# A fused sigmoid attention and token MLP on one core: a new order of steps, loads, casts and copies, seven casts on VectorE, one quadrant group fewer

## The chip, the cores and the metric

One core of a Trainium2 chip. The metric is the device time of one launch in microseconds (us): the median of several runs. Beside it stands the profile of one execution, whose span runs from the first to the last instruction.

## What is computed

Inputs are q, k, v of 8 batches, 12 heads, 448 tokens, head dimension 64 (fp32), and three weights. First comes attention with a sigmoid in place of the softmax, then a token-mixing MLP whose mixing weights are made from the attention's output:

```
attn  = sigmoid(q @ k.T / 8 - log(448))            # per batch and head
x     = (attn @ v) as [8, 448, 768]
wq, wk = x @ w_q, x @ w_k                          # hidden size 64
mixed = (wq @ wk.T / 8) @ x                        # per batch
out   = relu(mixed) @ w_out
```

The kernel computes in bf16 with fp32 sums and orders the MLP's products as wq @ (wk.T @ x), so that no 448 x 448 matrix is made there.

## The kernel before

**Units.** Four heads of one batch make a quad; there are 24 quads, three to a batch. A quad has 7 score steps, 168 in all. A score step is four 64x64-tiled matmuls of 448 columns on TensorE (line 121 records every matmul, line 124 every transpose), which fill one pair of PSUM banks, and one sigmoid of 128x896 on ScalarE (L331), which frees the pair and writes one of 16 slots of `at`. A value step multiplies one slot with `v` and sums into another pair; the seventh value step of a quad ends with a copy to `xt` (L355).

**From load to score.** SyncE issues the loads of q, k, v (448 KB each) and of w_out into a ring of six buffers `ld0` to `ld5`; a load goes out when the buffer's former content has been cast. Casts to bf16 run on GpSimd (L211 for q and k, L221 for v and the first q and k), a few on VectorE. Then q and k are transposed in one of three ways: on TensorE with a copy back by VectorE (L292, L300), or on VectorE alone. Of the latter, the plan letters `c` and `d` take one 128x448 STREAM_TRANSPOSE each for q and k (L271), after GpSimd has rearranged the cast tile with five copies (L167, L170, L173). The letters `r`, `s`, `z` do without the rearrangement: two 128x448 transposes (L264) and a quadrant group of four 32x448 ones (L251).

**MLP.** For each batch `xt` is transposed to `xn` (plan letters x, X, y, Y; X and Y as 7 whole 128x128 transposes, x and y as 28 of 64x64; y and Y with the copy by ScalarE, L384 or, in the tail, halves at L382); w and W multiply with w_q and w_k (the cast weights are `wqk`, four 64x384 casts, L754); N transposes the result to `wkn` (L449); U makes `tmp` (L462), M the mixed and rectified `mx` (L467, L469), O the output (copies at L601 and L646, the last at L599 and L555 in the function `middle`). w, X and part of O use all 128x128 cells, the rest 64x64 tiles.

**What sets the order.** All is written out by hand: `PLAN` is one letter per step (S score, P or p value step, the letters above, D one store of an output tile, C a copy of w_out to the other half, 1 the next cast that `ORDER` marks with a dot, on VectorE), `BANKS` gives the PSUM pair (0 to 3) or single bank (a to h) of each step that takes one, `ORDER` the order of the loads (q1 is quad 1's q; w0 are w_q and w_k, w1 to w6 are w_out). Each engine runs its instructions strictly in the order in which the plan issues them; a cast without a dot goes to GpSimd as soon as its buffers are planned free.

```
        if t in "12":
            cast_one("vs"[int(t) - 1])
            continue
```

Of the kernel before, what the change touches and what calls it, by code (L numbers as in the profile page):

```python
# [17 lines left out]
def kernel(  # L18
# [22 lines left out]
    NB = D // 2  # L41
# [6 lines left out]
    def pool(name, bufs, **kw):  # L48
# [15 lines left out]
    pairs = [banks[:, 2 * n : 2 * n + 2] for n in range(4)]  # L64
    pairs16 = [banks16[:, 2 * n : 2 * n + 2] for n in range(4)]
    BANKS = (
        "abcd0123200233111020302312031203101031021g2012020120h1g21320"
        "132123103103213012302g01h20h1g2031a32102312g12h1201321gh0210"
        "12h01210321g201321g2h01gh201g20132cd302c302302131e301230ef31"
        "0ef3102102c302d320d320123cd20gh120g102310g102hg102312gh10210"  # L70
        "ef130210ef1302120120320312321031021021321a310320321320120123"
        "020210320120c3210210312"
    )
    given = list("".join(BANKS))
    held = set()
# [1 line left out]
    def bank2():  # L77
        n = int(given.pop(0))
        assert not held & {2 * n, 2 * n + 1}
        held.update({2 * n, 2 * n + 1})  # L80
        return n, pairs[n], pairs16[n]
# [7 lines left out]
    def release(fb):  # L89
        gone = {2 * fb, 2 * fb + 1} if isinstance(fb, int) else {"abcdefgh".index(fb)}  # L90
        assert gone <= held
        held.difference_update(gone)
# [16 lines left out]
    def ld_next():  # L109
        nld[0] += 1  # L110
        return lds[(nld[0] - 1) % 6]
# [8 lines left out]
    def mm(*args, **kw):  # L120
        products.append(nc.tensor.matmul(*args, **kw))  # L121
# [6 lines left out]
    COPY = dict(v=nc.vector.tensor_copy, s=nc.scalar.copy, g=nc.gpsimd.tensor_copy)  # L128

    def xt(u, j):  # L130
# [5 lines left out]


    PLAN = (
        "SSFKESSES1EEqESDD1DESjPPppSpDpPDSSSqS1kSpPPSqSpSkSDPPSPSxSxr"
        "sSWwDDDDSSwzDPpSPppSpPSrSwSwWsSPpXSPNpSpPPSUSqSzMSSkpSpPpSMS"  # L140
        "ppPSSxSxMScPpSdPSpppSSPwWwrWSSXWDWSSosOSNPpPSpppzPSSOOSxSrPP"
        "ppSUSsppzPSoSOSoSoSppMpSPPPPSSWOWWWScSdxWODSMDWSOSxCOSMppScP"
        "DppSPPDSodDoSpxPDPDSCPrPSpDSPOOSNSsSOoDzOOSUSXcSPdpPSSpPPSPo"
        "OWSMSwowWMSSOwWCScpppSxpdpSpPSOoMSPPcDSPPpSpSPOoNSSSdDOoDOOp"
        "xDSPpPxSPpPDSuwcWwdSSMWOoSMSDwwOOSDxpPSPrPSmPpPDooNDSDSosoOz"
        "oSDDSxOOSUDpSDPPPDSPpcDSPoDODSSSodOoOSPMpSPPPSPPSwWwoScMSdOw"
        "wSSWOONSPMPcpSPPPPSSOodXSOSxoSoxSOppSpcUPSPpPSoOSdSxOOSPPPmp"
        "pPSPoSoMmOSOLScllLSLLSDodODSONxOPSpcpdpDPSPSPoOSoSOSOoSUSoSO"
        "SpPPpp1SoSOpSPOSOyppPMpPpplMlmlxlLlxOoONooUoOMmooOmooOoOOOOO"
        "oOOOOooOo"  # L150
    )
    PLAN = "".join(PLAN)
    KIND = ["a"] + [t for t in PLAN if t in "qacr"]
# [384 lines left out]
    def middle(w, us, k, part, fb, ps):  # L538

        x = part // 2  # L540
        for c in range(part % 2 * NC // 2, (part % 2 + 1) * NC // 2):
            for u in us:
                st = mxs[w].rearrange("p (c u s) -> p c u s", u=2, s=S)[:, c, u, 3 * NP : 4 * NP]
                mm(
                    ps[HALF[u], x, 0:NB], st, wout16[:, c, x * NB : (x + 1) * NB],
                    start=(c == 0), stop=(c == NC - 1),
                )
        if part % 2:
            if not x:
                ot[0] = ld_next()[:, 0:D]  # L550
            o = ot[0][:, x * NB : (x + 1) * NB]
            half = NB // 2
            for y in range(2):
                cols = slice(y * half, (y + 1) * half)
                COPY["vs"[y]](out=o[:, cols], in_=ps[:, x, cols])  # L555
            rows = out[2 * w : 2 * w + 2].rearrange("u (p i) d -> (u p) i d", i=NI)[:, NI // 2, x * NB : (x + 1) * NB]
            if x:
                for y in range(2):
                    (nc.sync, nc.scalar)[y].dma_start(out=rows[HALF[y]], in_=o[HALF[y]])
            else:  # L560
                nc.sync.dma_start(out=rows, in_=o)
        if part < 3:
            opened.append((w, us, k, part + 1, fb, ps))
        else:
            release(fb)

    def out_pair(act, tail):
# [7 lines left out]
        if len(us) == 2 and w == MIXED:  # L575
            middle(w, us, k, part, fb, ps)
            return
# [101 lines left out]
    def cols(r):  # L679
        return slice(r.start * HD, r.stop * HD)  # L680
# [8 lines left out]
        out=ident, in_=ident, compare_op=ALU.not_equal, fill=1.0, base=0,  # L689
# [4 lines left out]
    for _ in range(31):  # L694
# [1 line left out]


    ORDER = (
# [5 lines left out]
    )  # L704
    BEHIND = {}
    BY = {"s": [], "v": []}
# [76 lines left out]
    for t16, t32, r, e in (  # L783
# [3 lines left out]
            out=t16[:, r].rearrange("p i b d -> p b i d"),  # L787
            in_=t32[:, :, cols(r)].rearrange("p b (i d) -> p b i d", d=HD),
# [3 lines left out]
    def tr_part(nm, t16, r, e, tiled=False):  # L792
# [19 lines left out]
        out=k016[:, K3].rearrange("p i b d -> p b i d"), in_=k0[:, :, cols(K3)].rearrange("p b (i d) -> p b i d", d=HD),  # L812
# [10 lines left out]
    for t in PLAN:  # L823
        pump_loads()
        pump()
        if t in "EF":
            fb, ps, _ = bank2()
# [49 lines left out]
        elif kind == "C":  # L877
            for y in range(2):
                nc.sync.dma_start(
                    out=wout16[HALF[y], NC + 2 * c : NC + 2 * c + 2, :], in_=wout16[HALF[1 - y], 2 * c : 2 * c + 2, :],  # L880
# [5 lines left out]
        elif kind == "M":  # L886
            u, x = divmod(c, NC // 2)
# [42 lines left out]
```

## Time and profile before

| | |
|---|---|
| time, median of 3 runs | 186.0 us (185.35 to 186.64) |
| span of the profiled execution | 183.1 us |
| between that span and the median | 2.9 us |
| TensorE, matmuls | 170.9 us busy, 93% |
| ScalarE | 159.4 us, 87% |
| VectorE | 134.4 us, 73% |
| GpSimd | 117.1 us, 64% |
| granted TensorE clock | 1.00 |

The profiled execution has no timed run of its own; its span lies 2.9 us under the median. Busy shares are averages over stages with different limits. The rows of the profile name line, engine, operation, tile written and tiles read, then the count, the busy time and the mean of one; PE is TensorE's matmuls, PEld its weight loads, DVE VectorE, ACT ScalarE, POOL GpSimd, SP SyncE. The end of a matmul is modelled and matmuls overlap, so a PE row that shows no gap may still hide waits of a tenth or two of a microsecond; the starts of rows are measured.

### The profile page before, as it was taken

Reading aid. Unit: us, or ns where it says so; the run is one execution under the profiler, and the core shown is the slowest. Engines: PE = TensorE matmul, PEld = TensorE weight load, DVE = VectorE, ACT = ScalarE, POOL = GpSimd, SP = SyncE. Lnnn points to the kernel's source line nnn. Section 1 sums busy time; section 2 is a strip of 40 time slices with the busy share of each in tenths; the row PEclk is TensorE's granted clock in tenths of the full one; section 3 lists DMA queues with packets and bytes.
Section 4 is the critical chain, followed back from the end, with each engine's and each line's share of the span. In section 5 each row is a group of like instructions: output and inputs, shape, how many; then the busy total and the mean of one; then the engine's idle time right before and its main releaser. Section 6 shows DMA issues by size and latency. Waiting matters only on the chain.

```text
span 183.1 us, 8403 instructions
## 1 busy us (share of the span) xinstructions
PE 170.9 (93%) x3617; PEld 113.1 (62%) x3618; DVE 134.4 (73%) x205; ACT 159.4 (87%) x207; POOL 117.1 (64%) x156
## 2 busy tenths in 40 slices
PE   7887789899999999999999999999999999999990
PEld 7544435544564565555556546556788898888970
DVE  2545699988998898988758876789786885693310
ACT  4699999999999999999999999899989979964330
POOL 1228988998799996699999928999999400000000
PEclk9999999999999999999999999999999999999999
DMA  5999999969998769899889998997983333333686
GB/s 175 349 383 286 332 381 397 392 234 310 372 401 330 258 209 312 297 280 366 311 236 300 350 324 278 355 361 261 292 304 94 87 98 95 90 90 81 139 219 173
DMA packets 24261, 48.51 MB, mean 265 GB/s; under 512 B 3872, under 2 KB 16416, under 8 KB 24224
## 3 DMA queue, kind: packets, MB, share of 16 engines
q1 hardware_dynamic: 24000, 47.69, 78.4%
q8 instruction: 28, 0.46, 1.0%
q10 hardware_dynamic: 224, 0.30, 0.5%
q14 instruction: 9, 0.07, 0.1%
HBM read 35.78 MB, written 11.01 MB: 256 GB/s over the span
## 4 chain that ended last, share of the span: by engine, by line
PE 75%; ACT 13%; DMA 4%; issue 2%; DVE 2%; SPq 1%; ACTq 0%
PE banks L121 72%; ACT at L331 13%; DMA ld<-in_v_dram 4%; PE banks L124 4%; DVE xt L355 1%; DVE mx L469 1%; SPq L197 1%; DVE v L221 0%; DVE xn L384 0%; SPq L684 0%; SPq L682 0%; SPq L683 0%; DVE ld L555 0%; ACT ld L555 0%; ACTq L331 0%
## 5 line engine op out<-in xcount | busy, mean ns | idle before, releaser
L331 ACT ACTIVATE at<-banks 128x896 bf16<-128x896 f32 x168 | 141.1, 946 | 5.7 <-PE banks L121 5.2
L121 PE MATMUL banks<-wout,mx 64*64 64x384 bf16 (+2 forms) x816 | 66.2, 324 | 0.7 <-issue 0.6
L121 PE MATMUL banks<-qk 64*64 64x448 bf16 x672 | 61.5, 358 | 3.6 <-ACT at L331 2.8
L211 POOL CAST qk<-ld 128x896 bf16<-128x896 f32 x38 | 44.6, 1191 | 9.7 <-issue 7.3
L121 PEld LDWEIGHTS <-mx 64*64 64x64 bf16 (+2 forms) x816 | 39.6, 105 | 17.4 <-issue 6.9
L121 PE MATMUL banks<-at,v 64*64 64x448 bf16 x672 | 47.2, 351 | 0.9 <-ACT at L331 0.4
L121 PEld LDWEIGHTS <-qk 64*64 64x64 bf16 x672 | 27.1, 105 | 24.4 <-issue 18.0
L355 DVE CAST xt<-banks 128x896 bf16<-128x896 f32 x23 | 25.0, 1086 | 7.9 <-PE banks L121 6.0
L121 PEld LDWEIGHTS <-v 64*64 64x64 bf16 x672 | 23.7, 106 | 7.0 <-issue 1.4
L469 DVE TENSOR_SCALAR mx<-banks 128x896 bf16<-128x896 f32 (+1 forms) x21 | 19.9, 956 | 5.0 <-PE banks L121 4.2
L221 POOL CAST v<-ld 128x896 bf16<-128x896 f32 x22 | 20.7, 948 | 1.5 <-DMA ld<-in_v_dram 1.1
L271 DVE STREAM_TRANSPOSE qk<-qk 128x448 f32<-128x448 f32 x26 | 16.0, 630 | 0.1
L384 DVE COPY xn<-banks 128x896 bf16<-128x896 bf16 x21 | 13.1, 624 | 3.5 <-PE banks L124 2.6
L251 DVE STREAM_TRANSPOSE qk<-qk 32x448 f32<-32x448 f32 x24 | 15.3, 636 | 0.6
L170 POOL COPY qk<-qk 32x448 uint32<-32x448 uint32 x26 | 14.4, 554 | 1.6
L173 POOL COPY qk<-swap 32x448 uint32<-32x448 uint32 x26 | 14.4, 554 | 1.5
L121 PE MATMUL banks<-xt,wqk 64*64 64x448 bf16 (+1 forms) x84 | 13.8, 353 | 0.2 <-ACT at L331 0.2
L646 DVE COPY o<-banks 128x384 f32<-128x384 f32 x17 | 9.4, 553 | 3.4 <-PE banks L121 2.6
L124 PEld LDWEIGHTS <-xt 64*64 64x64 bf16 (+1 forms) x588 | 9.8, 108 | 3.1 <-issue 1.5
L124 PE MATMUL banks<-ident,xt 64*64 64x64 bf16 (+1 forms) x588 | 10.4, 194 | 0.2
L121 PE MATMUL banks<-wqk,tmp 64*64 64x448 bf16 (+3 forms) x72 | 8.7, 291 | 0.0
L121 PE MATMUL banks<-wq,tmp 64*64 64x448 bf16 (+2 forms) x72 | 8.4, 292 | 0.0
(67 smaller groups left out, 136.0 us busy)
## 6 DMA issues: line engine op xcount, KB each, us to landing
ld<-in_q_dram SPq DMA_DIRECT2D x24, 448.0 KB, 6.1
ld<-in_v_dram SPq DMA_DIRECT2D x24, 448.0 KB, 5.6
ld<-in_k_dram SPq DMA_DIRECT2D x23, 448.0 KB, 6.1
out_dram<-o SPq DMA_DIRECT2D x38, 192.0 KB, 4.9
out_dram<-ld SPq DMA_DIRECT2D x14, 192.0 KB, 2.8
ld<-in_moe_w_out_dram SPq DMA_DIRECT2D x6, 384.0 KB, 5.1
wout<-wout SPq DMA_DIRECT2D x6, 192.0 KB, 4.9
out_dram<-o SPq DMA_DIRECT2D x4, 96.0 KB, 1.9
```

The source lines that it names most:

```text
L121: products.append(nc.tensor.matmul(*args, **kw))
L124: products.append(nc.tensor.transpose(*args, **kw))
L170: eng.tensor_copy(out=w[lo, 1], in_=w[hi, 0])
L173: eng.tensor_copy(out=w[hi, 0], in_=z[lo])
L211: COPY[e](out=f[:, :, "qk".index(nm)].rearrange("p e i d y -> p e y i d"), in_=ld.pop((nm, n)).rearrange("p (y i e d) -> p e y i d", y=2, ...
L221: COPY[e](out=t16.rearrange("p i b d -> p b i d"), in_=ld.pop((nm, n)).rearrange("p b (i d) -> p b i d", i=NI),)
L251: nc.vector.transpose(out=qk[n][other : other + 32, h].rearrange("p t i n -> p (t i n)").bitcast(F32), in_=w[own : own + 32, 1 - h],)
L271: nc.vector.transpose(out=qk[n][:, t].rearrange("p t i n -> p (t i n)").bitcast(F32), in_=w)
L331: nc.scalar.activation(dst, src, ACTF.Sigmoid, bias=attn_bias, scale=attn_scale)
L355: COPY[eng](out=xt(u, j), in_=ps)
L384: COPY[eng](out=xn, in_=ps)
L469: nc.vector.tensor_scalar(dst, ps, moe_scale, 0.0, ALU.mult, ALU.max)
```

## The change

`PLAN`, `BANKS` and `ORDER` are written anew. Counted by letter: casts marked for VectorE go from four (q1, v0, k2, v23) to seven (q2, q3, w0, k19, v17, v18, v21); the quads with a quadrant group go from six to five (quad 17 is now of the kind c, d); three `xn` copies of the body (of batches 0, 5 and 6) go from VectorE to ScalarE (in the tail, behind the last score, each copy is split between the two whatever its letter); whole transposes (X, Y) from four to five, and 64x64 ones from 20 to 19; w and W are dealt anew, so that one pair of copies of `wq` leaves ScalarE for GpSimd. The letters S, P, D, M, N, U, C and the output steps stay the same in number. In the function `middle` the last two column halves of the output are no longer copied in two pieces each, one by VectorE and one by ScalarE; the first half is copied whole by VectorE, the second whole by ScalarE. Lines behind that place move up by three, so that L754 becomes L751, L601 L598, L646 L643.

```
-        "abcd0123200233111020302312031203101031021g2012020120h1g21320"
+        "abcd23001220113323310203120302301303c0312102g102012h0g123120"
...
-        "SSFKESSES1EEqESDD1DESjPPppSpDpPDSSSqS1kSpPPSqSpSkSDPPSPSxSxr"
-        "sSWwDDDDSSwzDPpSPppSpPSrSwSwWsSPpXSPNpSpPPSUSqSzMSSkpSpPpSMS"
...
+        "SSFKESSESEEqDESjSDSSS1SPqppPSPkPSPSPS1SppqSDkpPSpPSXSryESS1S"
+        "SswzDWppPpSpPPSwDDWSDSSwrWXpNSDPspDDpSPPPSUzSSSMSqkSpPSPDPMS"
...
-            half = NB // 2
-            for y in range(2):
-                cols = slice(y * half, (y + 1) * half)
-                COPY["vs"[y]](out=o[:, cols], in_=ps[:, x, cols])
+            COPY["vs"[x]](out=o, in_=ps[:, x, 0:NB])
...
-        ".q1 k1 .v0 .k2 q2 v1 q3 k3 q4 w0 k4 v2 k5 q5 v3 q6 k6 v4 k7 w5 "
-        "q7 v5 w3 q8 w1 k8 w2 w4 w6 v6 v7 q9 k9 k10 v8 q10 q11 v9 v10 "
-        "k11 k12 q12 v11 k13 q13 q14 v12 k14 v13 k15 q15 v14 k16 q16 k17 "
-        "v15 q17 k18 v16 q18 q19 v17 v18 v19 k19 k20 v20 q20 q21 v21 k21 "
-        "q22 k22 v22 k23 .v23 q23 "
+        "q1 k1 v0 .q2 k2 k3 v1 .q3 q4 k4 .w0 v2 k5 q5 v3 q6 v4 k6 w4 q7 "
+        "k7 v5 w5 k8 w1 q8 w2 w3 w6 v6 v7 k9 q9 q10 v8 k10 q11 v9 k11 q12 "
+        "v10 v11 k12 k13 q13 q14 k14 v12 v13 k15 q15 v14 v15 k16 q16 q17 "
+        "k17 q18 v16 k18 .k19 q19 q20 .v17 k20 k21 v19 q21 v20 .v18 v22 "
+        ".v21 k22 q22 k23 v23 q23 "
```

**First place: VectorE at the start, from the first cast of quad 1 on.** The numbers behind a tile's name count allocations; q16, k16, v16 are the cast tiles, `qk` the transposed ones, `ld` the load buffers. Before:

```order
L221 CAST q16_233<-ld2_102 128x2x7x64
L292 COPY qk_275<-banks_82 128x2x448
L221 CAST v16_286<-ld4_104 128x2x7x64
L292 COPY qk_275<-banks_82 128x2x448
L355 CAST xt0_90<-banks_82 128x2x7x64
L221 CAST k16_413<-ld5_105 128x2x7x64
```

Now:

```order
L292 COPY qk_278<-banks_82 128x2x448 x2
L221 CAST q16_342<-ld5_105 128x2x7x64
L300 COPY qk_435<-banks_82 128x2x2x448
L355 CAST xt0_90<-banks_82 128x2x7x64
L221 CAST q16_465<-ld3_103 128x2x7x64
L300 COPY qk_549<-banks_82 128x2x2x448
```

The casts q1, v0 and k2 have left for GpSimd, so that nothing stands between quad 1's two copies; q2 and q3 have come, each behind the copies of the quad before.

**Second place: VectorE from quad 4's transposes to the last quadrants of quad 5.** Before:

```order
L384 COPY xn_596<-banks_82 128x896 x2
L264 STREAM_TRANSPOSE qk_660<-qk16_453 128x448 x2
L251 STREAM_TRANSPOSE qk_660<-qk16_453 32x448 x4
L355 CAST xt2_92<-banks_82 128x2x7x64
L264 STREAM_TRANSPOSE qk_738<-qk16_560 128x448 x2
L429 CAST wqk0_96<-banks_82 128x448
L251 STREAM_TRANSPOSE qk_738<-qk16_560 32x448 x2
L384 COPY xn_596<-banks_82 128x896
L449 COPY wkn_802<-banks_82 128x448
L355 CAST xt3_93<-banks_82 128x2x7x64
L462 CAST tmp_831<-banks_82 128x384
L251 STREAM_TRANSPOSE qk_738<-qk16_560 32x448 x2
```

Now:

```order
L264 STREAM_TRANSPOSE qk_597<-qk16_468 128x448 x2
L751 CAST wqk16_84<-ld0_100 64x3x128 x4
L251 STREAM_TRANSPOSE qk_597<-qk16_468 32x448 x4
L355 CAST xt2_92<-banks_82 128x2x7x64
L264 STREAM_TRANSPOSE qk_736<-qk16_551 128x448 x2
L429 CAST wqk0_96<-banks_82 128x448
L384 COPY xn_583<-banks_82 128x896
L449 COPY wkn_768<-banks_82 128x448
L251 STREAM_TRANSPOSE qk_736<-qk16_551 32x448 x2
L355 CAST xt3_93<-banks_82 128x2x7x64
L462 CAST tmp_812<-banks_82 128x384
L251 STREAM_TRANSPOSE qk_736<-qk16_551 32x448 x2
```

The four casts of w_q and w_k now stand among quad 4's transposes; one of the two `xn` copies ahead of these has gone to ScalarE.

**Third place: ScalarE from its start to the first output copy.** Before:

```order
L786 CAST q16_154<-ld0_100 128x2x3x64
L801 COPY qk_161<-banks_82 128x3x2x64
L331 ACTIVATE at_89<-banks_82 128x896 x63
L646 COPY o_1449<-banks_82 128x384
L331 ACTIVATE at_89<-banks_82 128x896 x13
```

Now:

```order
L783 CAST q16_154<-ld0_100 128x2x3x64
L798 COPY qk_161<-banks_82 128x3x2x64
L331 ACTIVATE at_89<-banks_82 128x896 x20
L384 COPY xn_583<-banks_82 128x896
L331 ACTIVATE at_89<-banks_82 128x896 x43
L643 COPY o_1429<-banks_82 128x384
```

A copy of `xn` stands between the 20th and the 21st sigmoid, where before 63 sigmoids followed each other.

More of the change, by code (lines that the diff above doesn't have):

```diff
@@ L66 @@
     BANKS = (
[L67 to L72 removed]
+        "abcd23001220113323310203120302301303c0312102g102012h0g123120"
+        "321032103103123021302g01h20h1g2031a32102312g121h021301hg0210"
+        "12g01210321h201321gh201gh201320132cd302c302032101e031203e0f1"
+        "3ef1032102c302d302d302103cd02gh012g012312g102hg102312hg10210"
+        "ef130213fe1032120120320312321031021021321a310320321320120123"
+        "0201203201e0f1323021320"
     )
@@ L138 @@
     PLAN = (
-        "SSFKESSES1EEqESDD1DESjPPppSpDpPDSSSqS1kSpPPSqSpSkSDPPSPSxSxr"
-        "sSWwDDDDSSwzDPpSPppSpPSrSwSwWsSPpXSPNpSpPPSUSqSzMSSkpSpPpSMS"
[L141 to L150, printed above, removed]
+        "SSFKESSESEEqDESjSDSSS1SPqppPSPkPSPSPS1SppqSDkpPSpPSXSryESS1S"
+        "SswzDWppPpSpPPSwDDWSDSSwrWXpNSDPspDDpSPPPSUzSSSMSqkSpPSPDPMS"
+        "PpPSSxSxMSSPPPpcdSPPPSSWWWSSrXwWWsSSoDOSNPpSPPPSpzPSoOSxSprp"
+        "pPSCUSsPDpPzSOSOSSooSPMPSCcPDppSDpDPSwDwdoDSSxCOWWMSSwWOSxOS"
+        "MPPSPcPPSpPSODoSdPxpSppprDSpPSDsooNSSzSODOOOSUSScxpPDPSpPdpS"
+        "SPOOwSMSwWWOMSDSDwWOSpppSxPPcSpDPdSooSMppSPppcpSSPOoSNSSOOod"
+        "oxSppPxSpPDpPSuwDDwWcSSMoWdoWDSMSWooDSxppSPpPSmPPDocdoNSSo1c"
+        "ooS1SxOdOoPSPUSPPSpPPSOOSSSocOOoSPdMcpSpppPSDDPSo1DwDwWSMSOW"
+        "wSSWooNSMdP1pSpPpSPPSYOOSSOxoSOcxSOppSPpUSPPPdSoSoSxOOSppcDm"
+        "pPppSPOSoMmOSOLSdLLLlSLSoocSONyOpSPppDpDSpSoPOSoSDOSodoSUSDO"
+        "SOSpPPpSPPoSPoSOSOPPPxpMpplPLlMlmlLyXOOoNoOUOommOOoMOoOOOooO"
+        "oDooOOOooOo"
     )
```

## The prediction

> **What bounds the kernel now.** I read the page's first table, then the busy time by stage, then the engines' timelines around the places that the change touches. The stages (columns: length, then busy time and count of PE, PEld, DVE, ACT, POOL, the clock, the DMA share, GB/s):
>
> ```profile
> PE 170.9 (93%) x3617; PEld 113.1 (62%) x3618; DVE 134.4 (73%) x205; ACT 159.4 (87%) x207; POOL 117.1 (64%) x156
> 12.50:45.00 32.50, 27.89 (x671) 15.53 (x663) 26.47 (x36) 32.23 (x40) 28.75 (x34) 1.00 0.96 337
> 45.00:160.00 115.00, 114.90 (x2289) 74.05 (x2285) 93.78 (x139) 109.94 (x140) 85.57 (x113) 1.00 0.80 266
> 160.00:183.10 23.10, 18.12 (x490) 15.87 (x482) 8.96 (x18) 8.98 (x17) 0.00 (x0) 1.00 0.55 139
> 20.70:37.00 16.30, 14.18 (x327) 7.84 (x323) 15.75 (x23) 16.20 (x21) 14.37 (x18) 1.00 1.03 389
> ```
>
> Up to 45 us ScalarE is the bound: 32.23 busy of 32.50, with TensorE 4.6 us idle beside it. From 45 to 160 TensorE is: 114.90 of 115, ScalarE having 5.06 us and VectorE 21.2 us free. Behind the last sigmoid comes a tail of some 20 us of TensorE work. Within the first stage VectorE is as full as ScalarE between 20.7 and 37 us: 15.75 of 16.30. So the end moves by three things: when ScalarE's chain of sigmoids delivers the stage up to 45 us, how much work TensorE has after that, and the last copies.
>
> ScalarE's timeline carries the first of these:
>
> ```profile
> 6.50 5.78 ACT L331 ACTIVATE at<-banks 128x896 bf16<-128x896 f32 x7 [0.48 <-PE banks L121]
> 12.67 29.53 ACT L331 ACTIVATE at<-banks 128x896 bf16<-128x896 f32 x36 [0.40 <-PE banks L121]
> 155.27 4.21 ACT L331 ACTIVATE at<-banks 128x896 bf16<-128x896 f32 x5
> ACT at L331 <- PE banks L121: 4.3, 14, 0.9
> ```
>
> Thirty-six sigmoids in 29.53 us are 0.82 each, close to the 0.80 of the undisturbed row above (5.78 less about 0.95 for the last one, over six steps). Late loads thus cost this execution little: the gap ahead of 12.67, and about half a microsecond inside the 36. The last row, of the waits between 45 and 160 us, says that there ScalarE waits for TensorE, 4.3 us in 14 places, and not for loads.
>
> **The start.** The eighth sigmoid is late because of quad 1's second copy:
>
> ```profile
> 9.62 0.93 POOL L221 CAST k<-ld 128x896 bf16<-128x896 f32 x1 [2.50 <-DMA ld<-in_k_dram]
> 10.89 0.41 PE L124 MATMUL banks<-ident,k 64*64 64x64 bf16 x28
> 10.80 0.63 DVE L221 CAST v<-ld 128x896 bf16<-128x896 f32 x1 [0.52 <-DMA ld<-in_v_dram]
> 11.40 0.62 DVE L292 COPY qk<-banks 128x896 bf16<-128x896 bf16 x1
> 12.26 0.36 PE L121 MATMUL banks<-qk 64*64 64x448 bf16 x4
> ```
>
> k1 is cast at 10.55. Its transposes stood behind the seventh score (10.89), its copy behind the cast of v0 (11.40), the eighth score behind four value steps (12.26). The plan now puts the transposes ahead of the seventh score, v0 on GpSimd and the value steps later: transposes at 10.6, done at 11.0, copy from about 11.15 to 11.77, score at 11.8, sigmoid 0.41 later as before (12.26 to 12.67), at 12.2. That is **-0.45 us** for ScalarE's chain. Quad 1's q is cast 0.3 us later (0.93 on GpSimd for 0.63), but the sixth score behind it waits for a bank until 9.89 anyway.
>
> **What is put in its way.** Between the 20th and 21st sigmoid stands a copy of 128x896 on ScalarE, from PSUM. Its nearest row there, of the same size, is 922 ns, which on a full engine advances by 0.80 like the sigmoids; half the size takes 563 ns:
>
> ```profile
> L467 ACT ACTIVATE mx<-banks 128x896 bf16<-128x896 f32 x3 | 2.8, 922 | 0.0
> L382 ACT COPY xn<-banks 128x448 bf16<-128x448 bf16 x3 | 1.7, 563 | 0.0
> ```
>
> Nothing hides it, since the engine is full: **+0.80**, so that by ScalarE's own work its chain is 0.35 later.
>
> VectorE's chain beside it, from quad 4's transposes to quad 5's last quadrants, sets when the 36th score may start:
>
> ```profile
> 33.47 1.30 DVE L251 STREAM_TRANSPOSE qk<-qk 32x448 f32<-32x448 f32 x2
> 34.75 0.44 PE L121 MATMUL banks<-qk 64*64 64x448 bf16 x4 [0.43 <-ACT at L331]
> L786 DVE CAST q<-ld 128x512 bf16<-128x512 f32 x1 | 0.4, 426 | 2.5 <-DMA ld<-in_q_dram 2.5
> L811 DVE CAST k<-ld 128x256 bf16<-128x256 f32 x1 | 0.3, 293 | 0.4 <-DMA ld<-in_k_dram 0.4
> L384 DVE COPY xn<-banks 128x896 bf16<-128x896 bf16 x21 | 13.1, 624 | 3.5 <-PE banks L124 2.6 <-ACT at L331 0.6
> ```
>
> The quadrants end at 34.77 and the score starts at 34.75: no slack. Four casts of 64x384 come in (between 293 ns at 256 elements and 426 at 512, so 0.36 each, 1.44), one xn copy goes out (0.62): +0.8. VectorE's 0.55 us of idle time in that stretch takes part of it. N0 now stands ahead of the 30th score and right behind W and X, so TensorE waits for the copy L429 there; that adds 0 to 0.6. ScalarE's chain leaves this stage between 0.35 (its own work) and 1.4 later (0.8 and 0.6); I take **+0.6**, nearer the low end, since the two delays lie beside each other and TensorE's transposes fill most of N0's wait. The loads keep their pace: the sequence is as long and 1.03 of the DMA engines' time is used there now; q2 and q3 stand on VectorE where it waited for TensorE.
>
> **TensorE's work.** It is the same but for the switches between 64x64 tiles and the whole array:
>
> ```profile
> 62.13 0.57 PE L121 MATMUL banks<-qk 64*64 64x448 bf16 x8
> 62.54 0.39 PE L124 MATMUL banks<-ident,xt 64*64 64x64 bf16 x28
> 62.86 0.36 PE L121 MATMUL banks<-xt,wqk 128*128 128x448 bf16 x1
> 63.06 0.65 PE L121 MATMUL banks<-wout,mx 128*128 128x384 bf16 x3
> 63.64 0.38 PE L121 MATMUL banks<-qk 64*64 64x448 bf16 x4
> 62.71 0.22 PE banks L124 x28
> 60.98 0.65 PE L121 MATMUL banks<-wout,mx 128*128 128x384 bf16 x3
> 61.47 0.73 PE L121 MATMUL banks<-xt,wqk 128*128 128x448 bf16 x3
> 45.29 0.50 PE banks L124 x7
> ```
>
> Three whole matmuls of 384 columns take 0.49 (60.98 to 61.47); the score at 63.64 starts 0.58 behind their first, so 0.09 is the switch. The 28 transposes occupy 0.22 (the chain's row), the next whole matmul starts 0.32 behind the first of them: 0.10. Counted in the order of matmuls there are 84 switches before and 78 after; ahead of the last score 83 and 75. That is 8 x 0.1 = -0.8 by then. One transpose set more is whole (seven in 0.50, a switch in it, for 28 in 0.22) and lies behind the last score with its two switches: about +0.4. Sum **-0.4**, all on the path, as TensorE is full from 45 us on.
>
> **The last copies.**
>
> ```profile
> 178.77 0.36 DVE L555 COPY ld<-banks 128x192 f32<-128x192 f32 x1 [0.56 <-PE banks L121]
> 179.16 0.32 ACT L555 COPY ld<-banks 128x192 f32<-128x192 f32 x1 [0.60 <-DVE ld L555]
> L646 ACT COPY o<-banks 128x384 f32<-128x384 f32 x11 | 5.6, 505 | 0.1
> ```
>
> The two pieces run one behind the other, 178.77 to 179.48. One whole copy by ScalarE is 0.48 to 0.51: **-0.2**; the store behind it is the same.
>
> **What I cost at nothing.** ScalarE's further load in the body: two xn copies (1.6), two output copies more, one pair of wq copies (0.7) gone; it lies in the 5.06 us that ScalarE waits for TensorE. With that cover gone it is +1.7. The four late casts on VectorE (k19, v17, v18, v21; v-casts there take 0.62, k19 between that and GpSimd's 1.19) lie in 21.2 us of free time, and quad 17's four quadrant transposes, 636 ns each, leave. GpSimd gains five copies (2.8 us) and loses four casts (about 4). Behind a late v18 or v21 on VectorE the xt copy waits, and with it a PSUM pair; v18's load can go out when v17 is cast, twelve score steps ahead; v21's when k21 is, eight steps ahead, which at some 0.9 each and less k21's cast (1.19) leaves 6.0 us for the 5.6 that the row below has from issue to landing. So I see no wait, but at v21 only 0.4 to spare; a load later than that costs its excess. The wait for a store in the tail does not change.
>
> ```profile
> ld<-in_v_dram SPq DMA_DIRECT2D x24, 448.0 KB, 5.6
> ```
>
> **Sum.** -0.45 and the delays give +0.6; +0.6 - 0.4 - 0.2 = 0.0 on the span of 183.1, which lies 2.9 under the median: I forecast **186.0 us**, no change. One per cent, 1.9 us, is about what a measurement of this kernel can tell from no change. The forecast's own range is 184.9 to 187.2: the chain 0.35 to 1.4, and half a microsecond for waits that a new order moves.
>
> **Rivals.** *VectorE's casts wait for GpSimd's (slower).* A row speaks for it:
>
> ```profile
> 14.41 1.32 POOL L221 CAST v<-ld 128x896 bf16<-128x896 f32 x1 [0.16 <-DMA ld<-in_v_dram]
> 14.32 0.62 DVE L221 CAST k<-ld 128x896 bf16<-128x896 f32 x1
> 18.01 1.19 POOL L211 CAST qk<-ld 128x896 bf16<-128x896 f32 x1 [0.20 <-DMA ld<-in_moe_w_k_dram]
> ```
>
> GpSimd's cast took 1.32 instead of 0.93 while VectorE cast from SBUF beside it. The other way round is in no row. The four w0 casts now stand among GpSimd's casts in a stretch where that is 14.37 of 16.30 busy; were each held for half a GpSimd cast (0.6), VectorE's full chain would be 2.4 later, and the end at 186.0 + 2.4 = 188.4. It decides from 1.9, a wait of 0.5 for each. Against it: there GpSimd waits for loads too. The Trainium skill, page SBUF — State Buffer, section Who interferes with whom, has it that of a VectorE copy in a two-port mode and a GpSimd instruction the second to start blocks fully; by that rule each w0 cast could lose a whole GpSimd cast. The trace agrees for GpSimd as the loser (+0.39); no run here shows VectorE as the loser. *Faster:* TensorE's small waits go as well. The one of 0.61 us in the tail (row below) waits for nothing that the profile shows and may fall away, and so may the chain's delay of 0.6; with a third of ScalarE's 4.3 us in the body as well, 186.0 - 0.6 - 0.6 - 1.4 = 183.4. Against it: these waits follow TensorE, whose work stays.
>
> ```profile
> 165.24 1.00 PE L121 MATMUL banks<-wout,mx 64*64 64x384 bf16 x19 [0.61 <-issue]
> ```
>
> *The change does not do what it says:* loads were not late, and the new early order costs nothing: TensorE's sum and the last copies alone, 186.0 - 0.6 = 185.4.
>
> **How the numbers follow.** Forecast 0.52, VectorE held by GpSimd 0.19, faster 0.15, loads not late 0.14. Faster by over 1%: the third, 0.15. Slower: most of the second and a little of the first, 0.20. Within 1%: the rest, 0.65. The range reaches from 184.1 to 188.2: past the forecast's own bounds to the cheaper part of both outer rivals, so that about 2 in 10 are left out.
>
> **What would show it.** Right: the eighth sigmoid at about 12.2; the 21st at about 23.4 (thirteen steps of 0.80 and the copy) where 12.67 gave 23.1; the 43rd about 0.6 later than before; the last score's wait unchanged; one copy of 0.5 us at the end. The rival on ports shows as w0 casts longer than 0.36 or VectorE gaps between them. Wrong would be a new wait for a load on VectorE between 110 and 130 us, or TensorE idle behind N0.

## The result, and the profile after

192.89 us (191.12 to 194.11) where the kernel before took 185.93 (185.35 to 186.64): a ratio of 1.036 (1.032 to 1.040), **3.6 per cent slower**. The forecast was 186.0, its range ended at 188.2. The profiled execution has a span of 191.6 (183.1 before) and took 193.42 itself; so the two profiles lie 8.5 apart and the medians 7.0. Times here and below are medians of all runs of a kernel; the ratios leave out runs that lie over 1.5 per cent above its fastest.

The stages (length, busy and count of PE, PEld, DVE, ACT, POOL, clock, DMA share, GB/s), and three lines of the page's 40 slices:

```profile
12.50:45.00 32.50, 24.44 (x538) 13.58 (x538) 23.57 (x32) 27.00 (x35) 20.67 (x24) 0.89 0.84 293
45.00:160.00 115.00, 111.99 (x2208) 70.49 (x2211) 92.05 (x135) 109.77 (x141) 92.94 (x121) 1.00 0.83 273
160.00:191.60 31.60, 26.23 (x693) 22.71 (x685) 13.89 (x24) 16.76 (x26) 0.00 (x0) 1.00 0.52 128
...
PEclk9999985999999999999999999999999999999999
DMA  5999927996999999975899898379993344533675
```

Up to 45 us every engine is less busy than before (ScalarE 27.00, not 32.23), the clock is 0.89 and the DMA engines have a slice at 0.2 of their time. No engine became the bound there; all waited. ScalarE's timeline shows where:

```profile
11.54 9.07 ACT L331 ACTIVATE at<-banks 128x896 bf16<-128x896 f32 x11
22.29 2.54 ACT L331 ACTIVATE at<-banks 128x896 bf16<-128x896 f32 x3 [1.68 <-PE banks L121]
24.70 0.92 ACT L384 COPY xn<-banks 128x896 bf16<-128x896 bf16 x1
25.48 3.39 ACT L331 ACTIVATE at<-banks 128x896 bf16<-128x896 f32 x4
31.66 0.92 ACT L331 ACTIVATE at<-banks 128x896 bf16<-128x896 f32 x1 [2.79 <-PE banks L121]
33.15 0.92 ACT L331 ACTIVATE at<-banks 128x896 bf16<-128x896 f32 x1 [0.58 <-PE banks L121]
34.53 5.77 ACT L331 ACTIVATE at<-banks 128x896 bf16<-128x896 f32 x7 [0.46 <-PE banks L121]
...
146.50 0.92 ACT L331 ACTIVATE at<-banks 128x896 bf16<-128x896 f32 x1 [2.06 <-PE banks L121]
```

The seventh sigmoid starts at 11.54, the 18th at 22.29, the 25th at 31.66, the 147th at 146.50. The same sigmoid in both traces gives the account (changes of the difference, us; they add up to 8.5):

| from | what is there | change |
|---|---|---|
| start to the 1st | ahead of the first sigmoid | +0.24 |
| 1st to 8th | quad 1's copies | -0.58 |
| 18th | TensorE stands in k3's transposes | +1.97 |
| 21st | xn copy on ScalarE | +0.79 |
| 25th | TensorE waits for w_q, w_k | +2.96 |
| 26th, 27th | TensorE at half clock | +1.25 |
| 28th to 53rd, to 145th | | -0.43, -0.15 |
| 147th | TensorE stands a second time | +1.99 |
| to the last | | +0.13 |
| to the last copy's end | a stand of 0.94 gone, the last copies | -0.91 |
| last copy to end of span | the last two stores | +1.27 |

**The casts of w_q and w_k.** The chain of work that ended last runs through them (columns: start, length; pieces of 0.03 us and less left out); behind it the same four on VectorE's timeline, and GpSimd's:

```profile
25.35 1.08 DVE wqk L751
26.45 0.92 DVE wqk L751
27.40 1.09 DVE wqk L751
28.50 0.43 DVE wqk L751
```

```profile
25.27 3.65 DVE L751 CAST wqk<-ld 64x384 bf16<-64x384 f32 x4
...
23.79 2.37 POOL L211 CAST qk<-ld 128x896 bf16<-128x896 f32 x2 [0.22 <-DMA ld<-in_k_dram]
26.07 1.02 POOL L221 CAST v<-ld 128x896 bf16<-128x896 f32 x1
27.28 0.94 POOL L221 CAST q<-ld 128x896 bf16<-128x896 f32 x1 [0.19 <-ACT at L331]
```

GpSimd's casts end at 26.16, 27.09 and 28.22, VectorE's at 26.43, 27.37 and 28.49: each 0.27 behind. The fourth, with no cast beside it, takes 0.43. VectorE spends 3.65 us on what was put down as 1.44. The Trainium skill, page SBUF — State Buffer, section Who interferes with whom, says that of a VectorE copy or cast in a two-port mode and a GpSimd instruction the second to issue is blocked fully. This trace agrees, with VectorE as the loser.

In the kernel before GpSimd had made these four casts when TensorE came to the first product W:

```profile
19.36 2.17 POOL L754 CAST wqk<-ld 64x384 bf16<-64x384 f32 x4 [0.17 <-issue]
22.73 0.55 PE L121 MATMUL banks<-xt,wqk 128*128 128x448 bf16 x2
```

TensorE's timeline of the changed kernel behind its casts, and the clock by stretches:

```profile
28.98 0.55 PE L121 MATMUL banks<-xt,wqk 128*128 128x448 bf16 x1 [1.16 <-DVE wqk L751]
29.47 1.71 PE L121 MATMUL banks<-at,v 64*64 64x448 bf16 x16
30.96 0.58 PE L121 MATMUL banks<-qk 64*64 64x448 bf16 x4
...
26.50:28.70 2.20, 0.78 (x5) 0.20 (x4) 2.16 (x3) 2.20 (x3) 1.53 (x2) 0.75 0.01 2
29.00:34.80 5.80, 5.80 (x51) 2.08 (x52) 4.48 (x7) 2.11 (x3) 1.77 (x2) 0.53 0.81 275
```

The second product W stands ahead of sixteen value matmuls and the 25th score in TensorE's own order, so these wait too. The sixteen take 1.49 us (29.47 to 30.96), with the clock at 0.53 from 29.0 to 34.8. And the DMA engines move 2 GB/s from 26.5 to 28.7: SyncE's next load waits 7.4 us for the buffer that these casts free, and goes out at 28.95.

**TensorE's two stands** wait for nothing that the profile names:

```profile
19.23 0.38 PE L124 MATMUL banks<-ident,k 64*64 64x64 bf16 x25
21.39 0.22 PE L124 MATMUL banks<-ident,k 64*64 64x64 bf16 x3 [1.77 <-issue]
...
142.94 0.41 PE L124 MATMUL banks<-ident,xt 64*64 64x64 bf16 x26
145.04 1.17 PE L121 MATMUL banks<-wout,mx 64*64 64x384 bf16 x23 [1.56 <-issue]
...
q8 instruction: 28, 0.46, 0.9%
```

A set of 28 transposes is cut after 25. The last line is the queue that loads TensorE's program: 28 packets in 0.46 MB. Counted on the trace's matmuls and weight loads, the two stands come behind 703 and 5055 instructions, 17 x 256 apart, and end 1.41 and 1.28 us behind the landing of such a packet (19.98, 143.75).

**The end.** The last copies, then the issues of the last two stores, now and before:

```profile
185.35 0.56 DVE L552 COPY ld<-banks 128x384 f32<-128x384 f32 x1 [0.63 <-DMA out_dram<-ld]
186.27 0.48 ACT L552 COPY ld<-banks 128x384 f32<-128x384 f32 x1 [1.54 <-PE banks L121]
185.94 1.07 SPq L558 DMA_DIRECT2D out_dram<-ld  x1
187.10 0.91 SPq L556 DMA_DIRECT2D out_dram<-ld  x1
...
178.59 0.36 SPq L561 DMA_DIRECT2D out_dram<-ld  x1
179.51 0.49 SPq L559 DMA_DIRECT2D out_dram<-ld  x1
```

The issues took longer, so that the last store went out 0.35 us behind its copy (0.03 before) and landed later. From the last copy to the end of the span it is 4.88 us instead of 3.61. Of the other profiles in the new order a1, b2 and b4 have 4.8 to 4.9 there, and a3, a4, b3 and c4 3.9 to 4.1, as in the old order (3.6 to 4.0). What makes the issues long is open.

### The profile page after: what moved, and what is told of

It reads as the page before. It is cut to its first block, busy times and chain, and to the rows that moved or that the text cites. A ratio compares the mean times of both kernels' runs of the same rounds, so it can differ in the third digit from the quotient of the medians.

```text
span 191.6 us, 8367 instructions
## 1 busy us (share of the span) xinstructions
PE 172.6 (90%) x3597; PEld 113.8 (59%) x3597; DVE 134.0 (70%) x202; ACT 161.8 (84%) x208; POOL 118.3 (62%) x156
## 4 chain that ended last, share of the span: by engine, by line
PE 46%; POOL 20%; ACT 13%; issue 8%; DVE 7%; DMA 3%; POOLq 0%; DVEq 0%; ACTq 0%
PE banks L121 43%; ACT at L331 12%; POOL qk L211 9%; POOL qk L173 4%; PE banks L124 4%; POOL qk L170 3%; DVE wqk L751 2%; POOL swap L167 2%; DVE xt L355 2%; DMA ld<-in_k_dram 2%; DMA ld<-in_v_dram 2%; POOL v L221 2%; DVE qk L271 1%; DVE qk L292 1%; DVE xn L384 1%
## 5 line engine op out<-in xcount | busy, mean ns | idle before, releaser
L121 PE MATMUL banks<-qk 64*64 64x448 bf16 x672 | 62.2, 364 | 5.2 <-ACT at L331 3.6
L121 PEld LDWEIGHTS <-mx 64*64 64x64 bf16 (+2 forms) x816 | 39.3, 105 | 18.4 <-issue 7.4
L121 PE MATMUL banks<-at,v 64*64 64x448 bf16 x672 | 48.0, 360 | 0.2 <-POOL v L221 0.2
L221 POOL CAST v<-ld 128x896 bf16<-128x896 f32 x21 | 19.5, 937 | 7.9 <-PE banks L121 4.6
L271 DVE STREAM_TRANSPOSE qk<-qk 128x448 f32<-128x448 f32 x28 | 17.6, 633 | 1.0 <-POOL qk L173 0.9
L173 POOL COPY qk<-swap 32x448 uint32<-32x448 uint32 x28 | 15.9, 568 | 1.6
L170 POOL COPY qk<-qk 32x448 uint32<-32x448 uint32 x28 | 15.6, 556 | 1.7
L384 DVE COPY xn<-banks 128x896 bf16<-128x896 bf16 x18 | 11.2, 621 | 4.5 <-PE banks L124 4.5
L251 DVE STREAM_TRANSPOSE qk<-qk 32x448 f32<-32x448 f32 x20 | 12.7, 636 | 0.5
L598 DVE COPY ld<-banks 128x768 f32<-128x768 f32 x7 | 6.7, 957 | 4.9 <-PE banks L121 4.9
L643 DVE COPY o<-banks 128x384 f32<-128x384 f32 x15 | 8.2, 554 | 2.2 <-PE banks L121 1.8
```

What stands on the lines that cost most here:

```text
L170: eng.tensor_copy(out=w[lo, 1], in_=w[hi, 0])
L173: eng.tensor_copy(out=w[hi, 0], in_=z[lo])
L221: COPY[e](out=t16.rearrange("p i b d -> p b i d"), in_=ld.pop((nm, n)).rearrange("p b (i d) -> p b i d", i=NI),)
L251: nc.vector.transpose(out=qk[n][other : other + 32, h].rearrange("p t i n -> p (t i n)").bitcast(F32), in_=w[own : own + 32, 1 - h],)
L271: nc.vector.transpose(out=qk[n][:, t].rearrange("p t i n -> p (t i n)").bitcast(F32), in_=w)
L384: COPY[eng](out=xn, in_=ps)
```

## The experiments

Ratios are against runs of the kernel before that were made together with each experiment.

**The changed kernel again (a1).** No edit. 

> The changed kernel once more, nothing edited. Theory 'instructions': TensorE's two long stands that the profile puts down to nothing (1.77 us ahead of 21.39, 1.86 us ahead of 145.04) belong to the program: they lie on a multiple of 256 instructions of TensorE's stream from each other and come back at the same two instructions, each ended 1.3 to 1.4 us behind the landing of a 16 KB instruction block, with sizes between 1 and 2.2 us. Rival 'chance': they are a disturbance of one execution, and here one or both are gone, the span then 187 to 190 us instead of 191.6. Both: the 25th sigmoid about 4 us later against the 24th's step than in the kernel before, since the casts of w_q and w_k on VectorE take about 1.1, 0.9, 1.1 and 0.42 us again.

1.029 (1.024 to 1.034). Stands at the same two instructions (1.00 and 2.13 us) and a third at 44.05 (1.50): "instructions". The other part of the forecast missed: two casts of the weights were held (0.64, 0.92) and two not (0.42 each), and the 25th sigmoid lost 0.65 instead of about 4; no half clock followed. So the result's profile shows a costly execution of these casts.

**w_q and w_k back on GpSimd (a2).**

```
-... q4 k4 .w0 v2 ...        +... q4 k4 w0 v2 ...
-...ryESS1SSswz...           +...ryESSSSswz...
```

> The changed kernel with the four casts of w_q and w_k back on GpSimd, behind k4's cast; everything else of the change stays. Theory 'port': VectorE loses 3.65 us of held casts, the weights are ready at about 23.5 instead of 28.9, the 25th sigmoid's gap of 2.8 us goes and TensorE's clock stays whole, so that the 25th to 27th sigmoid come 4.2 us earlier: about 188.7 (187.9 to 189.5) where the changed kernel has 192.9. GpSimd's 2.2 us more lie in its waits (1.58 us ahead of 22.63, 4.6 us ahead of 32.85). Rival 'late load': the weights' load lands at 21.4 and the steps W that need it stand too early whoever casts; then the gap stays above 1.5 us and the time above 191. Rival 'order': nothing but the copy on ScalarE and the order of steps costs, and the time stays at 192 to 193.

188.96, 1.014 (1.009 to 1.018): "port", within its range, and 2.6 us under the changed kernel's repeat (191.57). "Late load" and "order" are out by their times. Since this takes the casts away altogether, it does not tell their being held from their standing on VectorE; the profiles below do.

**Boundaries moved (a3).**

```
-    for _ in range(31):  mm(... 0 : 132 ...)
+    for _ in range(62):  mm(... 0 : 66 ...)
```

> The changed kernel with 62 warm-up matmuls of 66 columns for the 31 of 132: as much work, 62 instructions of TensorE more ahead of everything, so that each boundary of 256 instructions falls 62 instructions earlier in the program. Theory 'instructions': the stand in k3's transposes at 21.39 and the one at 145.04 are no longer at these operations; what stands there are lies at other operations, again a multiple of 256 from each other; if both are gone the time is 3 to 4 us shorter, about 189.3, and if they move to other places it may be anything from 188.5 to 194. Rival 'place': the stands belong to the operations (k3's transposes waiting for something that the profile does not show), so they stay where they are, within 0.3 us, and the time stays at 192 to 193.5.

189.86, 1.021 (1.017 to 1.025). k3's transposes run through; TensorE stands in q3's (0.65) and within a score at 142.07 (1.34), again behind 702 and 5054 instructions, where other operations are now. So the stands belong to the count and not to the operations. All four casts were held here (1.13, 1.17, 0.90, 1.08).

**Zeros in the wait (a4).** Ahead of the first two products W:

```
+        if u == 0 and c < 2:
+            for d in range((3, 6)[c]):
+                mm(ps, zeros[:, 0:P], zeros[:, 0:S], start=(c + d == 0), stop=False)
-           start=(c == 0)
+           start=(c == 0 and u > 0)
```

> The changed kernel with nine matmuls of zeros (128x448, 0.19 us each at full clock, adding nothing to the sum) put into the wait for w_q and w_k: three ahead of the first product W, six between it and the second. The wait itself stays. Theory 'clock': TensorE's clock falls to half between 29.0 and 34.5 us because it stood from 24.9 to 29.0; with the wait filled the products of that stretch keep their full pace, the waits ahead of the 26th and 27th sigmoid (0.58 and 0.46 us) go, and the time falls by 1.0 to 1.3 us, to about 191.7. Rival 'wait alone': the half pace costs nothing since ScalarE has its own work, and the time stays within 0.3 us of 192.9, or rises by up to 0.5 where the zeros stand in the way.

189.82, 1.019 (1.015 to 1.023), clock 1.00 from 28 to 34 us. But in this profile none of the four casts was held (0.38, 0.42, 0.42, 0.42), so wait and clock are not told apart. d1 and d2 try it again.

**The kernel before again (b1).** No edit. 

> The kernel before once more, nothing edited, for a second profile. Theory 'instructions': TensorE's stands at multiples of 256 of its instructions are a property of how many loads and stores stand in the DMA queues when a block of instructions is asked for; in this kernel they are few, under 1.5 us in all (0.94 at 165.24 and 0.2 at 137.0 in the first profile), against 3.1 to 5 us in four profiles of the changed kernel and its variants. Rival 'chance': this profile has 3 us or more of them as well, and the stands explain none of the difference between the kernels.

Stands of 0.54, 0.32, 0.37, 0.48 and 0.70: 2.4 us as gaps, 1.9 without the 0.1 that a step takes. More than the 1.5 expected, less than in the changed kernel (3.6 and 4.3 by the same count).

**Loads held back (b2).** `BEHIND = {("k", 4): 224}` in the changed kernel. 

> The changed kernel with the load of k4, and so the loads behind it, held until the 224th matmul (15.0 to 15.5 us) instead of 12.0 to 12.3 us; the DMA engines have 3.5 us of loads in their queues then, so they do not run dry. Theory 'instructions wait behind loads': at 15.0 us, where TensorE's next block of 256 instructions is asked for, 3.5 us of loads are queued instead of 6.4, the block starts about 1.2 us behind the asking (as in the kernel before, 1.15) instead of 3.3 to 3.7, and the stand of 1.0 to 2.0 us in the 25th of k3's transposes is gone; the 18th sigmoid comes 0.8 to 1.9 us earlier. Since the weights' load lands no earlier than 20.7, part of it may be given back at the 25th sigmoid: time between 190.5 and 192.5. Rival 'TensorE's own pace': the 256 instructions with four transpose sets are simply used up too fast (4.4 us), the stand stays within 0.4 us, and the time is the same or higher.

189.43, 1.022 (1.015 to 1.028), better than the range. SyncE's timeline of the changed kernel, then of this one, then its TensorE:

```profile
12.24 0.34 SPq L189 DMA_DIRECT2D ld<-in_k_dram  x1
13.80 0.38 SPq L659 DMA_DIRECT2D ld<-in_moe_w_q_dram  x1
```

```profile
16.34 0.34 SPq L189 DMA_DIRECT2D ld<-in_k_dram  x1
16.78 0.77 SPq L659 DMA_DIRECT2D ld<-in_moe_w_q_dram  x1
...
20.33 0.39 PE L124 MATMUL banks<-ident,k 64*64 64x64 bf16 x28
20.55 0.55 PE L121 MATMUL banks<-at,v 64*64 64x448 bf16 x8
```

k3's 28 transposes run through. The instruction packet started 0.46 us behind the boundary ahead of it, where it had started 3.70 and 3.34 behind in the changed kernel's two profiles. That the packet waits behind loads is shown at this place, in one profile.

**w_q, w_k on GpSimd and the xn copy on VectorE (b3).** The edit above and `SryESSSS` to `SrxESSSS`. 

> The changed kernel with w_q and w_k cast on GpSimd (188.96 by itself) and, in addition, the copy of xn between the 20th and 21st sigmoid back on VectorE. Theory 'ScalarE full': without the casts VectorE has room for the copy's 0.62, the 21st sigmoid comes 0.8 earlier and nothing gives it back before the 43rd: 188.2. Rival 'VectorE full': the copy stands ahead of quad 4's transposes on VectorE, whose last quadrants then end 0.6 later and hold the 29th score: the time stays at 188.7 to 189.3.

187.97, 1.013 (1.005 to 1.020). The step from the 20th to the 21st sigmoid falls from 1.58 to 1.09 (0.80 is undisturbed) and is not given back: "ScalarE full" by the profile; the two times can't be told apart (1.014 and 1.013).

**Late casts back on GpSimd (b4)**, and the loads from q19 on in the old order:

```
-... k18 .k19 q19 q20 .v17 k20 k21 v19 q21 v20 .v18 v22 .v21 k22 q22 k23 v23 q23
+... k18 q19 v17 v18 v19 k19 k20 v20 q20 q21 v21 k21 q22 k22 v22 k23 v23 q23
```

> The changed kernel with the four late casts (k19, v17, v18, v21) back on GpSimd and the loads from q19 on in the order of the kernel before; the early part keeps the change. Theory 'late loads move the queue': in the changed kernel the last three loads go out 1.5 to 2.9 us later against the sigmoids than before and lie under the output's stores at 135 to 142 us, so that TensorE's block for the boundary at 143 to 145 us starts 3.7 us behind its asking and TensorE stands 1.9 to 2.1; with the old order that stand is under 0.6 and the time 1.3 to 2 us shorter, 190.9 to 191.6 on the 192.9 of the changed kernel. Rival 'GpSimd': these casts cost GpSimd 4 us where it is busy throughout, quad 19's to 22's transposes come later, and the time is 0.5 to 2 us longer.

196.91, 1.062 (1.055 to 1.070): "GpSimd", and worse than it said. VectorE's quad transposes wait 3.72 us for GpSimd (at 130.86), TensorE 3.48 for VectorE behind them. The second stand is gone, as the other theory said, but with TensorE waiting beside it that proves little. GpSimd has no room for these four in this order.

**The weights' casts alone, in the kernel before (c1).** `.w0`, and a 1 between `r` and `s`: `SxSxr1sSWw`. 

> The kernel before with one thing of the change alone: the four casts of w_q and w_k on VectorE, between quad 4's whole and quadrant transposes as in the changed kernel; loads and everything else as before. Theory 'port': GpSimd, rid of these casts, casts k4, v2, k5 and q5 in the same stretch; each cast of the weights that starts beside one ends about 0.3 us behind it, so that at least two of the four take 0.8 to 1.1 instead of 0.42; with the plain work (4 x 0.42) VectorE's chain is 2.2 to 3.5 us later at quad 4's last quadrants, TensorE waits at the first product W, and the time is 187.2 to 188.7. Rival 'no port': four casts of 0.42 each, 1.7 us on VectorE, of which its waits take 0.5: 186.5 to 187.1. Rival 'early enough': the weights land at 19.3 here and nothing downstream is held: 185.6 to 186.2.

190.25, 1.026 (1.019 to 1.032): this one edit costs 4.6 us. The chain from the second cast on, its shortest pieces left out, then TensorE's first two products W, and GpSimd:

```profile
24.25 1.25 DVE wqk L754
25.53 1.35 DVE wqk L754
26.90 0.93 DVE wqk L754
```

```profile
25.56 0.37 PE L121 MATMUL banks<-xt,wqk 128*128 128x448 bf16 x1 [2.96 <-DVE wqk L754]
27.87 0.56 PE L121 MATMUL banks<-xt,wqk 128*128 128x448 bf16 x1 [1.94 <-DVE wqk L754]
```

```profile
24.05 1.17 POOL L211 CAST qk<-ld 128x896 bf16<-128x896 f32 x1 [1.32 <-DMA ld<-in_k_dram]
25.43 1.18 POOL L211 CAST qk<-ld 128x896 bf16<-128x896 f32 x1 [0.21 <-DMA ld<-in_q_dram]
26.55 0.99 POOL L221 CAST v<-ld 128x896 bf16<-128x896 f32 x1
```

The first began at 23.86, before GpSimd's, and was free; the other three end 0.27 to 0.28 behind a GpSimd cast. "Port" as to the casts, but the range was too low by 1.6: it had VectorE's loss and not TensorE's 4.9 us of waiting in its own order for the first two products. Being held is the smaller part of that: the four took 3.95 us where four free ones take 1.7, so 2.3. The 22nd sigmoid comes 5.4 later; the other 3.1 come from where the casts stand, on VectorE from 23.86 on, when GpSimd had finished them at 21.53 in the kernel before.

**The start alone, in the kernel before (c2).** q1, v0 without a dot, the PLAN's first letters from the change. 

> The kernel before with the change's start alone: q1 and v0 cast on GpSimd, k1's transposes ahead of the seventh score, value steps behind the eighth; the remaining order, the loads' order and k2's cast as before. Theory: the eighth sigmoid at about 12.1 instead of 12.5 to 12.7, that is 0.4 to 0.6 earlier, kept at the 24th if no new stand of TensorE comes in: 185.3 where the kernel before has 185.9. Rival 'instructions': the transposes of quads 2 and 3 follow each other more closely, TensorE uses up its block of 256 instructions sooner while the loads' queue is as deep, and a stand of 0.5 to 1.5 us at 14 to 21 us takes the gain: 185.8 to 186.8.

186.32, 1.002 (0.999 to 1.006); the eighth sigmoid at 12.71. The rival's time, but not its reason: no stand over 0.4 us came. The first four value steps still stood ahead of the eighth score here, so the whole edit of the change was not tried; d3 does.

**Start, last copies, boundary moved, in the kernel before (c3).** c2's edit, `middle` as changed, 55 warm-up matmuls of 74 columns. 

> The kernel before with the change's start, the change's last copies, and 55 warm-up matmuls of 74 columns for the 31 of 132 (48 instructions more, so that the boundaries of 256 fall elsewhere; counted on the trace of the kernel before, the two shortest blocks between 125 and 150 us then take 4.5 and 4.7 us instead of 3.8 and 4.1). Theory 'sum of the good parts': 0.4 to 0.6 at the start, 0.2 at the end, and 0.4 to 1.0 of the small stands (0.37 and 0.48 at 133 and 138 us in the second profile): 184.6 (184.0 to 185.4). Rival 'stands come elsewhere': the boundary falls among other transposes, and the time stays at 185.5 to 186.5.

184.70, 0.996 (0.992 to 1.000): in the range of "the good parts", but the start's part did not come: from the first to the eighth sigmoid it took 6.20 us, as before (6.17).

**All three causes mended in the changed kernel (c4).** b3's edits, `BEHIND = {("k", 4): 248}`, 55 warm-up matmuls of 74 columns. 

> The changed kernel with all that cost it undone by small edits: w_q and w_k cast on GpSimd, the xn copy on VectorE (187.97 with these two), k4's load held until the matmul that is asked for at 15 us, and 48 instructions more ahead. Theory 'the three causes are all': the early stand (0.6 in that profile) and part of the late one (2.1) go, and the time is 185.9 to 187.0, level with the kernel before. Rival 'the order itself': what is left against the kernel before is not in these causes, and the time stays at 187.5 to 188.5.

186.57, in the range, where the kernel before had 185.69; the ratio is 1.000 (0.995 to 1.005). The 18th sigmoid's gap and the 25th's are gone; the late stand is still there (1.24 at 139.09).

**Clock apart from wait (d1, d2).** First c1's kernel again, then with 14 and 9 zero matmuls in the wait. 

> The kernel before with the four casts of w_q and w_k on VectorE once more, as the standard for the next run. By the row of the first time: 4.6 us over the kernel before, three of the four casts ending 0.27 to 0.3 us behind a cast of GpSimd, TensorE at half clock for about 4.5 us behind the wait.

> The same with TensorE's wait for these casts filled: 14 matmuls of zeros (128x448) ahead of the first product W, nine between it and the second, adding nothing to the sum; the wait itself stays. Theory 'clock': TensorE's clock stays whole, the sigmoids from the 23rd to the 25th come 0.80 apart instead of 1.3 and 1.5, and the time is 1.0 to 1.3 us under that of the standard. Rival 'wait alone': the time is within 0.4 us of the standard's.

189.76 and 188.78; 1.020 (1.015 to 1.025) and 1.017 (1.013 to 1.021). By stretches, d1 and then d2:

```profile
27.60:30.80 3.20, 3.20 (x38) 1.27 (x41) 1.99 (x4) 2.14 (x3) 0.08 (x1) 0.58 0.83 257
```

```profile
27.60:32.00 4.40, 3.84 (x55) 1.73 (x54) 3.14 (x6) 3.90 (x5) 0.01 (x1) 1.00 0.80 223
```

From the 22nd to the 25th sigmoid 2.41 us with zeros, that is 0.80 each; 2.96 without them, and 3.63 in c1. The half clock costs 0.55 to 1.2 in the profiles; the times lean that way without settling it (1.0 between the medians, 0.6 by the ratios, whose intervals overlap). In d1 two of the four casts were free and the four took 2.99 us, 0.96 less than in c1; the step to the 22nd sigmoid is 0.98 shorter (5.22 for 6.20). So what the casts are held for is passed on in full.

**Eighth score ahead of the value steps (d3, d4).** `jSSPPpppDpPD...` for c2's `jSPPppSpDpPD...`, and the same with c3's other edits. 

> The kernel before with q1 and v0 cast on GpSimd, k1's transposes ahead of the seventh score, and now also the eighth score ahead of the first four value steps. Theory of the prediction: the eighth sigmoid at 12.1 instead of 12.5 to 12.7 where k1's copy ends by 11.5, so 0.4 to 0.6 earlier, kept behind it: 185.2 where the kernel before has 185.7. Rival 'given back': the value steps are late by 0.4 to 0.8 then, quad 0's xt and the third quad's copies with them, and the gain is gone by the 30th sigmoid: 185.6 to 186.2.

> The same with the change's last copies and the 48 instructions more ahead (without the moved score 184.7, that is 1.0 under the kernel before). Theory: the start's 0.4 to 0.6 adds to it: 184.2 (183.7 to 184.9), or 0.8 per cent under the kernel before. Rival: the start is given back, 184.6 to 185.4.

d3: 0.999 (0.996 to 1.002). The eighth sigmoid comes at 12.10, as forecast, and the ninth at 13.40: given back one step later. d4: 184.97, **0.995 (0.992 to 0.998)**, inside both forecasts' ranges: 0.9 us under the kernel before, and so ahead of both kernels; from c3 (0.996) it can't be told apart. From the ninth sigmoid on it gains little over c3. The profiles show the gain of both in the tail, from the last sigmoid to the end of the last copy: 19.84 us in c3 and d4, 20.07 in d2, which has the old copies and no stand there, and 20.94 and 20.70 in the kernel before, with stands of 0.94 and 0.70. So both the last copies (about 0.25) and the moved boundary have a part.

## Why the prediction was wrong

- **The start, -0.45.** Right: -0.58. By itself it is worth nothing (d3). The changed kernel's profile keeps it up to the 17th sigmoid; that this is because the plan puts more value steps behind the eighth score is not shown.
- **The xn copy, +0.80.** Right: +0.79.
- **VectorE's four casts.** This is the step that failed, in the price and in who pays it. "0.36 each, 1.44" was 3.65, and "+0.6" for ScalarE's chain was +6.1 at the 43rd sigmoid, 4.2 of it here and 2.0 in TensorE's first stand. The rival had the mechanism and nearly the size on VectorE (2.4 later; 3.65 - 1.44 = 2.2), but got a chance of 0.19, against it that GpSimd waits for loads there too. Over the nine profiles with these casts on VectorE, 22 of 36 began beside a GpSimd cast, and every one of the 22 ended 0.27 to 0.28 behind it; the other 14 took 0.38 to 0.43. What neither had was who waits: the step looked at the 36th score, behind the quadrants, while the products W stand ahead of the 25th in TensorE's order (2.96), and its half clock followed (1.25). The loss at the 25th sigmoid follows the casts: 3.0 to 3.7 us in the three profiles of the new order in which the four took 3.65 to 4.3 (the result, a3, b4), 0.65 and 0.8 where they took 2.5 and 2.6 (a1, b2), none with the casts on GpSimd (b3, c4). So in the changed kernel most of it is their being held. By the times the edit costs 2.6 of the repeat's 5.3 us (a1, a2); in the old order it costs 3.8 to 4.6 (d1, c1), there mostly by where the casts stand.
- **"The loads keep their pace."** Wrong twice. w_k's load has ten loads ahead of it instead of nine and lands at 21.39, not 19.25, which held nothing, since VectorE came to the casts at 25.27; and the next load waits 7.4 us for a buffer that VectorE has yet to cast from.
- **TensorE, -0.4.** Wrong in sign as far as it can be measured. From the 53rd to the last sigmoid 64 switches became 58, as counted, but without its stands the stretch takes 109.3 to 109.5 (seven profiles in the new order) instead of about 108.8 to 109.1 (the nine in the old one). What small waits took the gain back is open. In the tail the further whole transposes cost 0.2 (20.03 in the new order, 19.84 in c3 and d4, which have the same last copies), half of what was put down.
- **The last copies, -0.2.** Right: 0.48 where two pieces took 0.71. But "the store behind it is the same" was not: +1.27, open as to its cause.
- **The late casts.** No wait for a load on VectorE between 110 and 130 us, as said; k19 and v18 took 1.0 and ended 0.5 behind a GpSimd instruction. But the last loads go out 1.4 to 2.6 us later against the sigmoids and lie beside the output's stores. That this makes the second stand fits what b2 shows of the first, and is not shown.
- **Not in the sum at all:** TensorE's stands for its own program, 1.97 and 1.99. The prediction saw the row of 0.61 in the tail, called it a wait for nothing and counted it in its rival as a gain; it is one of these, and did go here, while two larger ones came.

## What to carry to other kernels

Before a cast from SBUF to SBUF goes to VectorE, look at what GpSimd does in that stretch: if it casts back to back, each VectorE cast is priced at the rest of a GpSimd cast and 0.3 us (0.5 for the casts of 128x896, as v18), and what waits for it is read from the in-order queue of the engine behind, not from the chain that the edit was meant for. A row with "issue" on TensorE is worth counting in instructions: where it falls a fixed number of them past a multiple of 256 it moves with every edit ahead of it, and holding back loads that are not needed yet can remove it, as in b2.

## What the runs showed that was not expected

**TensorE waits for its program.** In seventeen profiles, those of both kernels and all above but a2, TensorE has 23 steps of 0.54 us or more from one matmul's start to the next (behind the first 9 us) that are put down to nothing. All 23 lie 190 or 191 instructions past a multiple of 256 and end 1.28 to 1.69 us behind the landing of a 16 KB packet. Over all 476 blocks the packet starts a median of 0.5 us behind the boundary ahead of it when under 50 KB of loads and stores are issued and not yet moved (56 blocks), and 2.9 when 1.6 MB or more are (42 blocks, though from -0.7 to 4.6). So a block that TensorE uses up in 4 to 4.5 us, as the two that end in the stands, comes late where the DMA queues are full. The Trainium skill, page Runtime: NRT & Kernel Launch, section Instruction fetch mechanics, gives blocks of 256 instructions, as here, and calls the cost mostly hidden; here it was up to 2.1 us a time.

**The clock falls without a full stop.** In the changed kernel's profile the clock is at half from 27.62 to 34.44 us. In the 3.4 us ahead of that TensorE was at work up to 25.3 and then did one score and one product W, with waits of 1.22 and 0.55 ahead of them. In all profiles the stretches at half clock between the start and the end of the work last 3.41 or 6.83 us. The Trainium skill, page TensorE: Matmul & The Clock Gate, Part 1, has it fall after an idle window of about 3.4 us; no wait here was that long.

**The new order loses the clock early in some executions.** In the repeat of the changed kernel:

```profile
13.10:16.10 3.00, 2.96 (x57) 1.99 (x60) 0.00 (x0) 2.42 (x3) 1.32 (x2) 0.50 1.05 391
```

The 12th sigmoid came 1.0 later for it. Of the eight profiles in the new order other than a2, four have such a stretch ahead of 18.4 us (a1, a4, b2, c4; a4 has two), and none of the nine in the old order. The old plan has four value steps ahead of the eighth score, but d3 and d4, which put them behind it, keep the clock; so why it falls is open.
